# Reordering two places in the engine queues of a fused attention and feed-forward kernel: a weight conversion in the first group, and the last forms of the ninth group

## The chip, the cores and the metric

The kernel runs on one core of a Trainium2 chip. A core has a matrix engine (TensorE, PE in the profile), a vector engine (VectorE, DVE), an activation engine (ScalarE, ACT), a general engine (GpSimd, POOL) and a queue engine (SyncE, SP) that mostly issues transfers. Each engine works off its own list of instructions; semaphores make one engine wait for another. The metric is the device time of one execution in microseconds (us).

## The reference: what is computed

```python
kv  = einsum('bhsd,bhse->bhde', k, v)           # per head, 64 x 64
out = einsum('bhsd,bhde->bhse', q, kv)          # q, k, v: (8, 8, 576, 64)
rms = sqrt(mean(out * out, axis=-1) + 1e-06)
x   = (out / rms * g_norm)  ->  (8*576, 8*64)   # 4608 tokens, 512 wide

h  = x @ w_in                                   # w_in:  512 x 2048
sp = maximum(h, 0) + log1p(exp(-abs(h)))        # softplus
g  = h * erf(sp)
y  = g @ w_out                                  # w_out: 2048 x 512
```

Attention without a softmax, a norm over each head's 64 values, and a feed-forward block with its own activation function. The two weight matrices arrive as 64-bit floats; everything else is 32-bit.

## The kernel before

**Groups.** The 4608 tokens are cut into nine groups of 512. Groups T = 0 to 7 are the first 512 rows of each batch element. What is left of each (64 rows) is gathered in `x_last` and makes the ninth group, T = 8 (`T == B` in the code). For each group the attention is done in four pairs of heads (p = 0 to 3), and the feed-forward block in 16 units of 128 columns of `w_in` (`FC = 16`).

**Attention** (`attention`, from L269) is cut into six pieces: `products` (kv and the transposed q), `apply` (q times kv), `halve` (a split of the squares), `mean` (the mean of squares on PE, then logarithm, exponential and square on ACT, L358 to L360), `norm` (three DVE instructions, L366, L369, L378) and `split`. For T = 8 there are no products; `square` reads `x_last`. The pieces of group T + 1 are placed by hand between the units of group T.

**Forms.** From the second group on, the products are made of cut operands[...]. `thirds` (L424) cuts a tile into an upper form (ACT, L405), a lower form, which is the rest (DVE, L408), and a mix of both (DVE, L411). `product` (L449) then needs 12 matmuls: eight into `n_ps` (upper and lower form for each of four blocks) and four into `m_ps` (the mix). It takes turns over three pairs of PSUM banks, so the result that lay in a pair must be read out before the product three places later writes there.

**First stage, n = 0 to 32** (L644): groups 0 and 1, one unit a step. In group 0 the 64-bit weights are converted. `weights()` (L256) does one step of it: `w_split` of one block (DVE L207 and L216, then ACT L215 and L219), `w_join` of the block before it (DVE L226, L230, L240) and the load of a later block. `due(k)` says whether a conversion is needed soon; `due(1)` asks for one more step in advance than `due(0)`. It is called in two places of a step: with 1 ahead of the attention pieces of that step, which include `norm`, and with 0 after them (L658 and L664). `gates` (L641) multiplies h by erf(softplus(h)). At n = 6 the first pair's `norm` of group 1 comes up.

**Second stage, m = 8 to 36** (L786): groups 2 to 8 in batches of four units. Pass m makes the four hidden products of batch m (`hidden`), then the four result products of batch m - 1 (`result`, L765). Around them it does the following in this order:

- for each of four units i: the hidden product; for the first two, the forms of the gated h of the batch before (`cut_upper` on ACT, `cut_lower` on DVE); then h is copied out of PSUM (ACT L836, and DVE L445 adds the second bank), and softplus (ACT L838);
- the error functions (ACT L842), and, when little is left in `todo`, a load of the softplus table (L843);
- for each of four row blocks j: the result product, which DVE adds to `e` (L440 and L445), and after j = 1 the gates of this batch on DVE (L856, two halves).

The attention pieces wait in the list `todo`; `places` says after which unit or row block each may run (1 to 4 are the units, 5 to 8 the row blocks). m = 31 is the last batch of group 7, in which the last pair of group 8 gets its `mean`, `norm` and `split`. m = 32 is the first batch of group 8, whose first product needs those forms. m = 35 is the last batch and m = 36 only makes results.

[...]

Of the kernel before, what the change touches and what calls it, by code (L numbers as in the profile page):

```python
# [43 lines left out]
AF = mybir.ActivationFunctionType  # L44
# [6 lines left out]
BATCH = 4  # L51
# [5 lines left out]
SHIFT = 4096.0  # L57
# [3 lines left out]
def kernel(  # L61
# [10 lines left out]
    nc = tc.nc  # L72
    P = 128
    B, H, S, D = q.shape
# [30 lines left out]
    def softplus_table():  # L105
        nc.scalar.preload_act_table_set("softplus")  # L106
# [149 lines left out]
    def weights():  # L256

        w_next("split")
        w_next("join")
        w_next("load")  # L260
# [183 lines left out]
    def add(out_, ps):  # L444
        nc.vector.tensor_tensor(out=out_, in0=ps, in1=out_, op=ALU.add)  # L445
# [45 lines left out]
    def w_lower(which, f):  # L491

        t, x, parts = w_new.pop((which, f))
        lower_w(x, *(parts[:, i] for i in range(3)))
        kept = w_kept[which, f] = dram.tile([P, 3, G], FP32, name=f"w_{which}{f}")
        for i in range(3):
            if t is None:
                nc.sync.dma_start(
                    out=kept[:, i].rearrange("p (c f) -> p c f", c=KC), in_=parts[:, i].bitcast(FP32)
                )  # L500
        if t is not None:
            nc.sync.dma_start(out=kept, in_=t.bitcast(FP32))
            if which == "in" and f >= WHOLE:
                w_now[which, f] = [t]

    def hidden(T, f, turns=True):

        w = w_now["in", f].pop(0).rearrange("p i (c f) -> p i c f", c=KC).bitcast(FP32R)
        x = x_forms[T]
        return product(lambda form, c: w[:, form, c], lambda form, c: x[form][:, c], turns)  # L510


    NB = FC // BATCH
# [35 lines left out]
    def unit(name):  # L549
        return gate.tile([P, G], FP32, name=name, tag=name[0])  # L550
# [30 lines left out]
    first_batch, batches = FIRST * NB, NG * NB  # L581
# [5 lines left out]
    def load_parts(which, n):  # L587


        pool = w_out_p if which == "out" and len(w_seq["out"]) > BATCH else w_in_p  # L590
        for _ in range(n):
            if w_seq[which]:
                key = w_seq[which].pop(0)
                t = pool.tile([P, 3, G], FP32, name=f"w_{which}_parts", tag="w")
                nc.sync.dma_start(out=t, in_=w_kept[key])
                w_now.setdefault(key, []).append(t)


    def pieces_of(T):


        steps = [([], [], []) for _ in range(FC)]
        for p in range(NP):
            products, apply, halve, mean, norm, split = attention(T, p)
            f = (BATCH - 1) * (p + 1) if T < FIRST else BATCH * p

            steps[f][2 if T == FIRST or p == 1 else 1].append(products)
            steps[f + 1][1].append(apply)
            steps[f + 2][0].append(halve)
            with_erf = (f + 2) % BATCH == BATCH - 1  # L610

            place = 2 if T < FIRST and p == 0 else 1
            steps[f + 2][place].append(partial(mean, table=not with_erf))
            steps[f + 3][0].append(norm)
            steps[min(f + 4, FC - 1)][0].append(split)
        return steps
# [18 lines left out]
    def due(k):  # L635

        i = w_at["join"] + k
        ahead = 1 if LAG - 2 <= n < LAG + BATCH else 2
        return i < len(w_order) and w_order[i][0] <= n + ahead
# [4 lines left out]
    for n in range(FIRST * FC + 1):  # L644
# [10 lines left out]
        if T < FIRST:  # L655
            if f == 0:
                steps = pieces_of(T + 1)
            if due(1):  # L658
                weights()
            for key in list(w_new)[:2]:  # L660
                w_lower(*key)
            for piece in steps[f][0]:
                piece()
# [13 lines left out]
        if T == FIRST - 1 and f >= WHOLE:  # L677
            n_ps, m_ps = hidden(T, f, turns=False)
# [19 lines left out]
        if T < FIRST:  # L698
            if n == whole:
                old_h = acc.tile([P, BATCH, G], FP32, name="h", tag="e")  # L700
            h = hs[n] = old_h[:, n - whole] if n >= whole else unit("h_sb")
# [51 lines left out]
    def part(h, half):  # L753
        return h[:, :, half * 2 * P : half * 2 * P + 2 * P]

    def cut_upper(h, half):

        t = late_r.tile([P, 3, BATCH, 2 * P], FP32R, name=f"g_forms{half}")
        upper(part(h, half), t[:, 0])
        return t  # L760

    def cut_lower(h, half, t):
        lower(part(h, half), *(t[:, i] for i in range(3)))

    def result(T, b, j, g, w):  # L765

        ps = product(
            lambda form, f: g[j // 2][:, form, f, j % 2 * P : j % 2 * P + P],
            lambda form, f: w[f][:, form],
        )  # L770
        if b == 0:
            if j == 0:
                all_e = wide.tile([P, J, DM], FP32, name="e", tag="a")
                es.update((i, all_e[:, i]) for i in range(J))
            nc.vector.tensor_scalar(
                out=es[j], in0=ps[0], scalar1=SHIFT - 1.0, scalar2=None, op0=ALU.mult
            )
        else:
            add_scaled(es[j], ps[0], SHIFT - 1.0)
        add(es[j], ps[1])  # L780
# [5 lines left out]
    for m in range(first_batch, batches + 1):  # L786
        T, b = divmod(m, NB)
        todo = []
        if T + 1 < NG:
            todo = list(attention(T + 1, b))  # L790
            if b == 0:
                side = late_r if T % 2 == FIRST % 2 else late
                forms = side.tile([P, 3, KC, G], FP32R, name=f"x_forms{(T + 1) % 2}")
                x_forms[T + 1] = [forms[:, i] for i in range(3)]

        def piece():
            if todo:
                todo.pop(0)()


        places = (0, 2, 3, 5, 6, 8)
        if T + 1 == B:
            places = (0, 0, 0, 5, 6, 7)
            if b == NB - 1:

                places, todo[3] = (0, 0, 0, 4, 5, 6), partial(todo[3], table=False)
        elif b == NB - 1:
            places = (0, 2, 3, 5, 6, 7)

        def pieces(place):  # L810
            while todo and places[-len(todo)] <= place:
                todo.pop(0)()

        def fetch(place):
            for which in FETCH[place].split():
                load_parts(which, 1)

        pieces(0)
        g, done = g_next, len(g_next)
        g_next = []  # L820
        if m < batches:

            pool, tag = (acc, "e") if m % 2 else (wide, "b")
            h = pool.tile([P, BATCH, G], FP32, name="h", tag=tag)
            s = gate_r.tile([P, BATCH, G], FP32, name="s", tag="s")
        for i in range(BATCH):
            if m < batches:
                n_ps, m_ps = hidden(T, b * BATCH + i)
            fetch(i)
            if i == 0:  # L830
                for half in range(done, 2):
                    g.append(cut_upper(old_h, half))
            if done <= i < 2:
                cut_lower(old_h, i, g[i])
            if m < batches:
                nc.scalar.activation(h[:, i], n_ps, AF.Copy, scale=SHIFT - 1.0)  # L836
                add(h[:, i], m_ps)
                nc.scalar.activation(s[:, i], h[:, i], AF.Softplus)  # L838
            pieces(i + 1)
        if m < batches:  # L840
            for i in range(2):
                nc.scalar.activation(part(s, i), part(s, i), AF.Erf)  # L842
            if len(todo) < 3:  # L843
                softplus_table()
        T2, b2 = divmod(m - 1, NB)
        w = [w_now["out", b2 * BATCH + f].pop(0).bitcast(FP32R) for f in range(BATCH)]
        for j in range(J):
            result(T2, b2, j, g, w)
            fetch(BATCH + j)
            if b2 == NB - 1:  # L850
                store(T2, j, es.pop(j))
            if j == 1 and m == batches - 1:
                cut_lower(h, 0, g_next[0])

            for half in range(2) if j == 1 and m < batches - 1 else (j,) if j < 2 and m == batches - 1 else ():
                nc.vector.tensor_tensor(  # L856
                    out=part(h, half), in0=part(h, half), in1=part(s, half), op=ALU.mult
                )
            if j == 0 and m == batches - 1:
                g_next.append(cut_upper(h, 0))  # L860
            pieces(BATCH + 1 + j)
        old_h = h
# [33 lines left out]
```

## Time and profile before

| | |
|---|---|
| time, median of 3 runs | 948.07 us (947.21 to 948.4) |
| span of the profiled execution | 945.7 us |
| PE busy | 926.8 us (98%) |
| DVE busy | 740.5 us (78%) |
| ACT busy | 615.7 us (65%) |
| hidden products, n_ps and m_ps from x_forms | 233.2 + 120.0 us on PE |
| result products, n_ps and m_ps from g_forms | 231.2 + 124.2 us on PE |
| table loads on ACT | 44, of 1283 ns |

The rows of a timeline read: start, length, engine, line, operation, output <- inputs, shape, count, and in brackets the idle time of the engine just before, with what ended it. Consecutive instructions of one kind are merged into one row. Starts are measured; the ends of matmuls are modelled and overlap the next, so PE's pace is read from the distance between two starts. "Lnnn" is a line of the code.

### The profile page before, as it was taken

To read this page: it belongs to the slowest core of one execution; us is meant where nothing else is said; L and a number is where in the kernel's file an instruction comes from. 1 tells how busy PE (TensorE), PEld (TensorE's weight loads), DVE (VectorE), ACT (ScalarE), POOL (GpSimd) and SP (SyncE) were. 2 spreads that over 40 slices of the span, in tenths; PEclk is the share of its full clock that TensorE was granted. 3 is DMA by queue.
4 is the path that set the end of the run, shared out by engine and by line. 5 is a ranking of instruction groups with operands and counts; after the bars stand their busy time and mean duration, and the time that the engine had idled before them with its cause. 6 is when DMAs were issued, how large, how long until landed. Compare 5 with 4: busy or idle time off the path is not lost.

```text
span 945.7 us, 11743 instructions
## 1 busy us (share of the span) xinstructions
PE 926.8 (98%) x4272; PEld 683.3 (72%) x4272; DVE 740.5 (78%) x1054; ACT 615.7 (65%) x825; POOL 2.4 (0%) x10
## 2 busy tenths in 40 slices
PE   6999999999999999999999999999999999999998
PEld 4444445665688888888888888888888888878886
DVE  3979958888578788777788888878887877777667
ACT  3889876777666666666666666666666666665552
POOL 1000000000000000000000000000000000000000
PEclk9999999999999999999999999999999999999999
DMA  9856505899699998998899889998896778768872
GB/s 258 282 158 215 169 9 215 310 339 340 219 364 346 317 303 284 315 301 303 275 295 314 303 288 311 312 301 294 293 323 261 265 247 352 284 245 309 335 273 60
DMA packets 111842, 259.78 MB, mean 275 GB/s; under 512 B 43864, under 2 KB 69544, under 8 KB 111784
## 3 DMA queue, kind: packets, MB, share of 16 engines
q1 hardware_dynamic: 110152, 256.73, 78.4%
q10 hardware_dynamic: 1568, 2.29, 0.8%
q8 instruction: 34, 0.56, 0.2%
q14 instruction: 24, 0.20, 0.1%
q0 software_dynamic: 64, 0.00, 0.0%
HBM read 224.40 MB, written 34.60 MB: 274 GB/s over the span
## 4 chain that ended last, share of the span: by engine, by line
PE 88%; ACT 5%; DVE 5%; DMA 1%; issue 1%; DVEq 0%
PE n_ps L462 45%; PE m_ps L462 23%; PE o_ps L520 8%; PE h_ps L691 3%; PE se_ps L325 3%; PE kv_ps L297 2%; PE qt_ps L319 2%; ACT w_e L215 1%; ACT w_m L219 1%; DMA q_sb<-in_q_dram 1%; PE ms_ps L347 1%; PE ms_ps L346 1%; PE ms_ps L351 1%; ACT L103 1%; ACT s_sb L719 1%
## 5 line engine op out<-in xcount | busy, mean ns | idle before, releaser
L462 PE MATMUL n_ps<-x_forms,w_in_parts 128*128 128x512 f32 x896 | 233.2, 402 | 1.6 <-DVE x_forms L408 0.7
L462 PE MATMUL n_ps<-w_out_parts,g_forms 128*128 128x512 f32 x928 | 231.2, 391 | 0.0
L462 PEld LDWEIGHTS n_ps<-w_out_parts,g_forms 128*128 128x128 f32 x928 | 174.2, 188 | 38.4 <-issue 1.7
L462 PEld LDWEIGHTS n_ps<-x_forms,w_in_parts 128*128 128x128 f32 x896 | 166.7, 188 | 45.3 <-issue 9.1
L838 ACT ACTIVATE s<-h 128x512 f32<-128x512 f32 x112 | 71.0, 634 | 180.4 <-DVE h L445 180.4
L445 DVE TENSOR_TENSOR h<-m_ps,h 128x512 f32<-128x512 f32 x116 | 79.8, 688 | 60.9 <-ACT h L836 41.5
L462 PE MATMUL m_ps<-w_out_parts,g_forms 128*128 128x512 f32 x464 | 124.2, 389 | 0.0
L462 PE MATMUL m_ps<-x_forms,w_in_parts 128*128 128x512 f32 x448 | 120.0, 390 | 0.0
L520 PE MATMUL o_ps<-w_out_sb,h_sb 128*128 128x512 f32 x224 | 100.8, 593 | 0.3 <-DVE h_sb L642 0.3
L462 PEld LDWEIGHTS m_ps<-w_out_parts,g_forms 128*128 128x128 f32 x464 | 87.1, 188 | 18.1
L462 PEld LDWEIGHTS m_ps<-x_forms,w_in_parts 128*128 128x128 f32 x448 | 84.1, 188 | 17.7
L445 DVE TENSOR_TENSOR e<-m_ps,e 128x512 f32<-128x512 f32 x116 | 80.3, 692 | 18.3 <-PE m_ps L462 11.2
L440 DVE SCALAR_TENSOR_TENSOR e<-n_ps,e 128x512 f32<-128x512 f32 x88 | 60.3, 686 | 39.6 <-PE n_ps L462 39.6
L520 PEld LDWEIGHTS o_ps<-w_out_sb,h_sb 128*128 128x128 f32 x224 | 42.3, 190 | 48.9 <-issue 46.6
L411 DVE SCALAR_TENSOR_TENSOR g_forms<-g_forms 128x1024 fp32r<-128x1024 f32 x58 | 71.1, 1225 | 2.0
L408 DVE TENSOR_TENSOR g_forms<-h,g_forms 128x1024 fp32r<-128x1024 f32 x58 | 70.6, 1218 | 1.7 <-ACT g_forms L405 1.4
L836 ACT ACTIVATE h<-n_ps 128x512 f32<-128x512 f32 x112 | 65.5, 585 | 3.9 <-PE n_ps L462 3.8
L405 ACT ACTIVATE g_forms<-h 128x1024 fp32r<-128x1024 f32 x58 | 58.8, 1058 | 12.4 <-PE m_ps L462 9.8
L856 DVE TENSOR_TENSOR h<-h,s 128x1024 f32<-128x1024 f32 x56 | 66.0, 1218 | 0.7 <-ACT s L842 0.7
L691 PE MATMUL h_ps<-xT,w_in_sb 128*128 128x512 f32 x144 | 64.9, 594 | 0.8 <-DVE w_in_sb L240 0.6
L106 ACT ACT_TABLE_LOAD x44 | 56.5, 1283 | 0.7
L842 ACT ACTIVATE s<-s 128x1024 f32<-128x1024 f32 x56 | 56.3, 1053 | 0.3
(98 smaller groups left out, 1014.3 us busy)
## 6 DMA issues: line engine op xcount, KB each, us to landing
w_out_parts<-w_out SPq DMA_DIRECT2D x116, 768.0 KB
w_in_parts<-w_in SPq DMA_DIRECT2D x112, 768.0 KB
w_in<-w_new SPq DMA_DIRECT2D x16, 768.0 KB
q_sb<-in_q_dram SPq DMA_DIRECT2D x32, 256.0 KB
w_raw<-in_moe_w_out_dram SPq DMA_DIRECT2D x8, 1024.0 KB
out_dram<-e SPq DMA_DIRECT2D x32, 256.0 KB
k_sb<-in_k_dram SPq DMA_DIRECT2D x28, 287.5 KB
v_sb<-in_v_dram SPq DMA_DIRECT2D x28, 287.5 KB
```

Source lines behind the costliest of these rows:

```text
L106: nc.scalar.preload_act_table_set("softplus")
L405: nc.scalar.activation(high, x, AF.Copy, scale=1.0 + 2.0**-13)
L408: nc.vector.tensor_tensor(out=low, in0=x, in1=high.bitcast(FP32), op=ALU.subtract)
L411: nc.vector.scalar_tensor_tensor(out=both, in0=low.bitcast(FP32), scalar=SHIFT, in1=high.bitcast(FP32), op0=ALU.mult, op1=ALU.add,)
L440: nc.vector.scalar_tensor_tensor(out=out_, in0=ps, scalar=scale, in1=out_, op0=ALU.mult, op1=ALU.add)
L445: nc.vector.tensor_tensor(out=out_, in0=ps, in1=out_, op=ALU.add)
L462: nc.tensor.matmul(ps, lhsT=weights(form, k), rhs=moving(form, k), start=(form == forms[0] and k == 0), stop=(form == forms[-1] and k == 3),)
L520: nc.tensor.matmul(o_ps[j], lhsT=g[:, j * P : j * P + P], rhs=w_out_sb[:, f, :], start=(f == 0), stop=last,)
L691: nc.tensor.matmul(plain[i], lhsT=w_in_sb[:, c, i % FC * P : i % FC * P + P], rhs=xT[T][:, c, :], start=(c == 0), stop=(c == KC - 1),)
L836: nc.scalar.activation(h[:, i], n_ps, AF.Copy, scale=SHIFT - 1.0)
L838: nc.scalar.activation(s[:, i], h[:, i], AF.Softplus)
L856: nc.vector.tensor_tensor(out=part(h, half), in0=part(h, half), in1=part(s, half), op=ALU.mult)
```

## The change

It moves work inside the queues; its aim is that instructions which nothing holds up go ahead of instructions that wait for another engine.

- In step n = 6 of the first stage, `weights()` is called by the rule that before applied only after the attention pieces. So one conversion goes ahead of the first pair's `norm`.
- In pass m = 31, `norm` goes from after the first to after the second row block, and `split` after the third, where it now stands ahead of the load of the softplus table and ahead of the gates. The gates go from after the second to after the third row block.
- In pass m = 32 the first unit's h is copied out before the forms of the batch before are cut.
- The condition for the gates is rewritten. Before, passes with m < batches - 1 gated both halves, m = batches - 1 one half each after the first two row blocks, and m = batches none. Now every pass other than m = batches - 1 takes the last branch.

```diff
-            if due(1):
+
+            if due(0 if n == 2 * (BATCH - 1) else 1):
                 weights()
...
             if b == NB - 1:
 
-                places, todo[3] = (0, 0, 0, 4, 5, 6), partial(todo[3], table=False)
+
+                places, todo[3] = (0, 0, 0, 4, 6, 7), partial(todo[3], table=False)
+                todo[5] = partial(chain, todo[5], softplus_table)
...
+        to_last = m == B * NB - 1
...
+            def evacuate():
+                nc.scalar.activation(h[:, i], n_ps, AF.Copy, scale=SHIFT - 1.0)
+                add(h[:, i], m_ps)
+
+
+            early_copy = i == 0 and m == B * NB
+            if early_copy:
+                evacuate()
...
             if m < batches:
-                nc.scalar.activation(h[:, i], n_ps, AF.Copy, scale=SHIFT - 1.0)
-                add(h[:, i], m_ps)
+                if not early_copy:
+                    evacuate()
                 nc.scalar.activation(s[:, i], h[:, i], AF.Softplus)
...
-            if len(todo) < 3:
+            if len(todo) < 2:
                 softplus_table()
...
-            for half in range(2) if j == 1 and m < batches - 1 else (j,) if j < 2 and m == batches - 1 else ():
+            if m == batches - 1:
+                due_halves = (j,) if j < 2 else ()
+            else:
+                due_halves = range(2) if j == (2 if to_last else 1) else ()
+            if to_last:
+                pieces(BATCH + 1 + j)
+            for half in due_halves:
                 nc.vector.tensor_tensor(
                     out=part(h, half), in0=part(h, half), in1=part(s, half), op=ALU.mult
                 )
```

## The prediction

> **What bounds the kernel now.** I read the page's shares first, then the timeline of TensorE (PE) for the places where it stands still, then the other two engines' timelines at those places.
>
> ```profile
> PE 926.8 (98%) x4272; PEld 683.3 (72%) x4272; DVE 740.5 (78%) x1054; ACT 615.7 (65%) x825; POOL 2.4 (0%) x10
> ```
>
> PE is busy for all but 18.9 us of a 945.7 us span. The table of busy time by stage has it busy for the whole of every stretch from 100 to 250 us and 300 to 750 us, so an edit can pay only where PE stands still. Of the 18.9 us, 8.7 lie in the first 25 us and 4.5 after the last matmul's turn begins to run out (925 us on). The rest is small, and two pieces of it lie beside the change. The first is in group 0:
>
> ```profile
> 64.83 3.60 PE L691 MATMUL h_ps<-xT,w_in_sb 128*128 128x512 f32 x8
> 69.44 0.43 PE L324 MATMUL kv_ps<-qT_last,bd_kv 128*128 128x64 f32 x2 [1.02 <-DVE bd_kv L312]
> ...
> 74.30 3.70 PE L691 MATMUL h_ps<-xT,w_in_sb 128*128 128x512 f32 x8
> ...
> 86.02 0.80 PE L297 MATMUL kv_ps<-v_sb,k_sb 116*64 116x64 f32 x20 [0.29 <-DVE qT L366]
> 86.75 0.33 PE L305 MATMUL kv_ps<-ident,q_last 128*128 128x128 f32 x1
> 87.53 0.66 PE L319 MATMUL qt_ps<-ident,q_sb 128*128 128x128 f32 x4 [0.45 <-DVE xT L378]
> ```
>
> In brackets stands the idle time and what ended it: three times PE waits for VectorE (DVE). What DVE was doing:
>
> ```profile
> 56.03 0.69 DVE L642 TENSOR_TENSOR h_sb<-h_sb,s_sb 128x512 f32<-128x512 f32 x1
> 61.48 0.69 DVE L366 SCALAR_TENSOR_TENSOR qT<-ms_ps,qT 128x512 f32<-128x512 f32 x1 [4.76 <-ACT qT L360]
> ...
> 62.93 0.75 DVE L378 SCALAR_TENSOR_TENSOR xT<-se_ps,gm_col,qT 128x512 f32<-128x512 f32 x1
> 63.60 0.69 DVE L207 TENSOR_SCALAR w_e<-w_raw 128x1024 int32<-128x1024 int32 x1
> ...
> 68.33 0.68 DVE L642 TENSOR_TENSOR h_sb<-h_sb,s_sb 128x512 f32<-128x512 f32 x1
> 68.93 0.45 DVE L312 COPY bd_kv<-kv_ps 64x64 f32<-64x64 f32 x2
> ```
>
> It stood 4.76 us in front of the norm (L366), which needs ScalarE's (ACT's) logarithm, exponential and square. Only then came the weight conversion (L207 to L240, 63.60 to 68.33), and behind it the copy bd_kv that PE waits for. The second place is the first product of group 8:
>
> ```profile
> 840.92 1.54 PE L462 MATMUL n_ps<-x_forms,w_in_parts 128*128 128x512 f32 x6
> 843.18 0.49 PE L462 MATMUL n_ps<-x_forms,w_in_parts 128*128 128x512 f32 x1 [0.72 <-ACT x_forms L405]
> 844.42 0.50 PE L462 MATMUL n_ps<-x_forms,w_in_parts 128*128 128x512 f32 x1 [0.74 <-DVE x_forms L408]
> ```
> ```profile
> 839.17 2.01 ACT L842 ACTIVATE s<-s 128x1024 f32<-128x1024 f32 x2
> 841.20 1.28 ACT L106 ACT_TABLE_LOAD   x1
> 842.50 0.63 ACT L405 ACTIVATE x_forms<-x 128x512 fp32r<-128x512 f32 x1
> ```
>
> The upper form of the last attention piece waits behind a table load on ACT, and its lower form waits on DVE for the gates (two L856, 841.41 to 843.68). The third place is the end:
>
> ```profile
> 937.58 0.69 DVE L445 TENSOR_TENSOR e<-m_ps,e 128x512 f32<-128x512 f32 x1
> 938.19 0.68 DVE L440 SCALAR_TENSOR_TENSOR e<-n_ps,e 128x512 f32<-128x512 f32 x1
> ...
> 941.28 0.69 DVE L445 TENSOR_TENSOR e<-m_ps,e 128x512 f32<-128x512 f32 x1 [0.21 <-PE m_ps L462]
> ```
>
> DVE ends the work at 941.97. It is idle for only 0.71 us between the last two result blocks.
>
> [...] L207 had nothing to wait for at 56.7 and still ran at 63.60, behind the norm. [...] The trace has 1283 ns, and no drain (the load from 841.20 is followed by work at 842.50), so I use 1.28. [...] The row of L856 has 1218.
>
> **The change part by part.**
>
> *Conversion ahead of the norm (n = 6).* Compared with before, only DVE's order changes: L207, L216, L226, L230, L240 go in front of L366, L369, L378. The five start 0.60, 0.60, 1.14, 1.25 and about 1.14 us apart, 4.73 in all, and fit the hole: from 56.7 to 61.4, while the norm can start at 61.48. Does something else hold them? The two joins need ACT's L215 and L219 of the split before (54.91 to 57.0, done by the time L226 comes up at 57.9). The raw block was loaded three conversions earlier (issue at 42.70). Nothing holds them, and the norm isn't later. Behind the norm, the gates and bd_kv no longer have 4.73 us in front of them: bd_kv then waits for PE's own kv_ps (ends 64.4) and is done at about 65.1, where PE needs it at 68.4. ACT gains as well: L215 of the new split waited 1.57 us for L207 and now follows its table load at 62.75. Following both queues on to n = 9, ACT's square ends at about 81.7 instead of 85.25, and the norm of the second pair ends at about 83.9 instead of 87.47. PE would reach kv_ps at about 84.5 and qt_ps at 85.3. All three waits fall away. What they cost I take from PE's pace against the same pair of rows without a wait: L691 to L324 4.61 against 3.43 (1.18); the rows after it 0.10 and, up to the L691 of 74.30, 0.24; slower first matmuls after that 0.11; L691 to L297 3.89 against 3.52 (0.37); L305 to L319 0.78 against 0.16 (0.62). Sum 2.6. The bounds are 1.0 (the first wait alone) and 2.7; I take 2.5. PE shows no idle time from there to 250 us, and DVE and ACT, fed by PE, move with it.
>
> *Last forms of group 8 (m = 31 and 32).* No instruction is added there. On DVE the second result block (e, L440 and L445) goes ahead of the norm, into its 2.63 us wait for ACT; the norm still runs from 837.89 to 840.1. Then come the third block (to 841.4), the forms, the gates, the fourth block. On ACT the upper form follows the error functions directly: 841.20 to 841.83, and the table load comes after it. DVE's lower form then runs from 841.86 to 842.54, the third form to 843.27. PE wants the upper at 842.28, the lower at 842.51 and the third form at about 843.5: a loss of 0.1 instead of now 0.90 and 1.01 by pace, with 0.3 more for the slower matmuls after it (the next product's halves come 1.94 apart, not 1.81). So 2.2 less 0.1: 2.1 gained. What is pushed back: the gates end at about 845.5 (before: 843.7) and the fourth block's first half at 846.15. Its PSUM bank is the one that the third product of m = 32 writes from 846.4 on, 0.25 us of slack. The early copy of h serves that: the copy sits on ACT at 843.1, before the conversions of the gates, and its addition on DVE ends at 847.6. After that the additions and copies that free banks come 0.5 to 1 us ahead of PE (third copy 854.1, wanted at 854.6). Bounds for the gain: 1.0, if these slacks are eaten, and 2.2.
>
> *Gates in the last pass (m = 36).* The rewritten condition leaves out the old bound m < batches - 1, so the last pass multiplies the old h by s once more. Two L856-like instructions stand on DVE after the second result block, at 938.19. A pair takes 2.27 (841.41 to 843.68). Queued behind them are the third and fourth blocks and their stores. Third block 940.46, fourth 941.85 to 943.33, where the end was 941.97: 1.36 later, 2.27 less the 0.91 us of idle time that it absorbs. Nothing hides it, and the last store follows directly. Bounds 1.1 and 1.6 (the last two stores come closer together).
>
> Sum: 2.5 + 2.1 - 1.4 = 3.2 us. 948.07 - 3.2 = 944.9.
>
> **The rivals.**
> - *The group-8 gain is eaten by bank waits.* PE meets late evacuations in m = 32, and only 0.6 remain: 948.07 - 2.5 - 0.6 + 1.4 = 946.4. For it: slacks of 0.25 and 0.5 us in an order that I worked out by hand. Against: each is positive, and DVE idles 1.18 us twice before additions there.
> - *The group-0 gain is given back in group 1*, where the transfers of the cut weights fill the DMA engines (mean share 0.95 from 200 to 250 us) and PE waits 0.31 for DVE at 250.77: 948.07 - 2.1 + 1.4 = 947.4. Against: the DMA engines idle from 135 to 145 us and run at 0.40 from 250 to 260, so that stream is started by PE and would start earlier too.
> - *Both gains go and the added gates stay:* 948.07 + 1.4 = 949.5. It needs both rivals at once, in full; the removed waits are on PE itself, which speaks against it.
>
> **How the numbers follow.** Forecast 0.78, first rival 0.09, second 0.09, slower 0.04. The forecast's bounds are 948.07 - 2.7 - 2.2 + 1.1 = 944.3 and, with a gain of 1.0 in one of the two places and 1.6 at the end, about 946.4. Half a microsecond for the spread of the three times (947.21 to 948.4) makes 943.8 to 946.9, which holds the first rival too and leaves out 0.13. Faster by over 0.2% means below 946.2: nearly all of the forecast and some of the first rival, 0.80. Within: 0.16. Slower: 0.04.
>
> **What would show it.** Right: no PE wait for bd_kv near 68 us nor for L366 and L378 near 84; DVE's wait before L366 in group 0 near zero; the first L462 row of group 8 in one piece of eight; two gates on DVE some 5 us before the end, with the last addition starting about 5.1 us after the start of the second block's last addition (now 3.7). Wrong: a new PE wait on L440, L445 or the copy of h in m = 32; PE idle near 250 us grown by 2 us; or gates at the end that fall into idle time.

## The result and the profile after

| | before | after |
|---|---|---|
| time, median | 947.81 us (947.21 to 948.4, 4 runs) | 944.32 us (943.95 to 944.94, 4 runs) |
| span of the profiled execution | 945.7 us | 942.4 us |
| PE busy | 926.8 us | 924.8 us |
| DVE busy | 740.5 us | 742.6 us |

The changed kernel is 3.5 us faster; the ratio of the times is 0.9964, with a 95% interval of 0.9947 to 0.9981. The number of matmuls is the same in the two executions (4272), and DVE has 2.1 us more work. In the table of the kernel before, the 44 table loads are those of one line, L106 (softplus); with those ahead of the logarithm (L103, 33 times) and of the error function (L842 28 and L726 8 times in the kernel before) there are 113, of 1283 ns each, in both kernels. PE's busy time isn't a measure of the gain: it falls by 2.0 us with the same matmuls, since their ends are modelled and PE is 0.66 us less busy in the first 25 us, ahead of any difference between the kernels.

Three places account for it. In each I measure the distance between two rows of the same execution, because the start of the kernel is not equally long each time (last section). The first is group 0, PE's timeline after:

```profile
55.93 1.02 PE L351 MATMUL ms_ps<-qT,mean_w 128*128 128x512 f32 x2
...
64.98 3.60 PE L692 MATMUL h_ps<-xT,w_in_sb 128*128 128x512 f32 x8
68.41 0.33 PE L324 MATMUL kv_ps<-qT_last,bd_kv 128*128 128x64 f32 x2
...
72.93 3.60 PE L692 MATMUL h_ps<-xT,w_in_sb 128*128 128x512 f32 x8
...
84.18 0.80 PE L297 MATMUL kv_ps<-v_sb,k_sb 116*64 116x64 f32 x20
...
85.08 0.60 PE L319 MATMUL qt_ps<-ident,q_sb 128*128 128x128 f32 x4
85.51 3.60 PE L520 MATMUL o_ps<-w_out_sb,h_sb 128*128 128x512 f32 x8
```

All brackets are gone. Before, the stretch that I measure lies between these two rows:

```profile
55.78 1.02 PE L351 MATMUL ms_ps<-qT,mean_w 128*128 128x512 f32 x2
...
88.02 3.60 PE L520 MATMUL o_ps<-w_out_sb,h_sb 128*128 128x512 f32 x8
```

L692 (L691 before) to L324 is 3.43 us where it was 4.61. From the mean's matmuls in front (L351) to the L520 that follows qt_ps it takes 32.24 us before and 29.58 after: 2.66 gained. The three brackets of before add up to 1.76 only. A bracket counts from the modelled end of the matmul before it, and without a wait that end lies 0.07 to 0.17 us behind the next start (64.98 + 3.60 against 68.41), so each bracket misses that much. Some matmuls just after a wait are slower: the L691 at 74.30 takes 3.54 us to the next row (77.84), and 3.43 after. And there is a fourth wait, which stands on the weight load (PEld) of the L691 at 74.30, before:

```profile
74.30 0.30 PEld L691 LDWEIGHTS h_ps<-xT,w_in_sb 128*128 128x128 f32 x2 [0.91 <-DVE w_in_sb L240]
```

PE waits there for the weight itself, the end of the next conversion (L240, 73.02 to 74.24 on DVE). From the L520 ahead of it to this L691 it is 3.67 us before (70.63 to 74.30), and 3.43 after (69.50 to 72.93). DVE's timeline after shows why the waits are gone:

```profile
55.96 0.68 DVE L642 TENSOR_TENSOR h_sb<-h_sb,s_sb 128x512 f32<-128x512 f32 x1
56.56 0.68 DVE L207 TENSOR_SCALAR w_e<-w_raw 128x1024 int32<-128x1024 int32 x1
...
60.15 1.23 DVE L240 TENSOR_TENSOR w_out_sb<-w_e,w_m 128x1024 f32<-128x1024 f32 x1
61.42 0.69 DVE L366 SCALAR_TENSOR_TENSOR qT<-ms_ps,qT 128x512 f32<-128x512 f32 x1
...
63.55 0.68 DVE L642 TENSOR_TENSOR h_sb<-h_sb,s_sb 128x512 f32<-128x512 f32 x1
64.60 0.46 DVE L312 COPY bd_kv<-kv_ps 64x64 f32<-64x64 f32 x2 [0.37 <-PE kv_ps L297]
```

The conversion fills the 4.76 us in which DVE stood, the norm still runs at 61.4, and the copy bd_kv now waits for PE and no longer PE for it. The next conversion moves up as well: its L207 is at 65.09 where it was at 69.42.

The second place is the first product of group 8. PE, then ACT, then DVE, after:

```profile
838.42 1.98 PE L462 MATMUL n_ps<-x_forms,w_in_parts 128*128 128x512 f32 x8
840.25 1.09 PE L462 MATMUL m_ps<-x_forms,w_in_parts 128*128 128x512 f32 x4
841.17 2.00 PE L462 MATMUL n_ps<-x_forms,w_in_parts 128*128 128x512 f32 x8
...
843.91 1.98 PE L462 MATMUL n_ps<-x_forms,w_in_parts 128*128 128x512 f32 x8
```
```profile
836.60 2.01 ACT L856 ACTIVATE s<-s 128x1024 f32<-128x1024 f32 x2
838.51 0.61 ACT L405 ACTIVATE x_forms<-x 128x512 fp32r<-128x512 f32 x1
839.15 1.28 ACT L106 ACT_TABLE_LOAD   x1
```
```profile
839.16 0.69 DVE L408 TENSOR_TENSOR x_forms<-x,x_forms 128x512 fp32r<-128x512 f32 x1 [0.24 <-ACT x_forms L405]
839.89 0.69 DVE L411 SCALAR_TENSOR_TENSOR x_forms<-x_forms 128x512 fp32r<-128x512 f32 x1
840.50 2.35 DVE L876 TENSOR_TENSOR h<-h,s 128x1024 f32<-128x1024 f32 x2
```

Eight matmuls in one row, where before six, one and one stood with 0.72 and 0.74 us between them. The upper form now precedes the table load, the other forms precede the gates. From this product to the third one it takes 7.68 us before (840.92 to 848.60) and 5.49 after (838.42 to 843.91): 2.19 gained. The row of the third one before:

```profile
848.60 1.98 PE L462 MATMUL n_ps<-x_forms,w_in_parts 128*128 128x512 f32 x8
```

The third is the end. PE's last row before and after, then DVE after:

```profile
940.17 1.07 PE L462 MATMUL m_ps<-w_out_parts,g_forms 128*128 128x512 f32 x4
```
```profile
935.49 1.07 PE L462 MATMUL m_ps<-w_out_parts,g_forms 128*128 128x512 f32 x4
```
```profile
932.88 0.69 DVE L445 TENSOR_TENSOR e<-m_ps,e 128x512 f32<-128x512 f32 x1
933.49 2.35 DVE L876 TENSOR_TENSOR h<-h,s 128x1024 f32<-128x1024 f32 x2
...
937.94 0.69 DVE L445 TENSOR_TENSOR e<-m_ps,e 128x512 f32<-128x512 f32 x1
```

The two gates of the last pass stand in front of the last two result blocks, and the waits for PE there (0.71 and 0.21 us) are gone. From PE's last m_ps to the last addition it takes 1.11 us before (940.17 to 941.28) and 2.45 after (935.49 to 937.94): 1.34 lost.

The sum is 2.66 + 2.19 - 1.34 = 3.51, and the medians differ by 3.49. That the two agree so closely is luck. The three profiled kernels without the conversion's move take 32.02 to 32.24 us for the stretch of group 0, and those with all of it 29.57 or 29.58, so the gain there is 2.4 to 2.7. In group 8 it is 7.62 to 7.70 without the new order and 5.49 to 5.57 with it: 2.05 to 2.21 gained. The traces thus give 3.1 to 3.5 us, and the spans of the two executions differ by 3.3.

### The profile page after: what moved, and what is told of

Same layout as the page of the kernel before. It is cut to its first block, busy times and chain, and to the rows that moved or that the text cites. A ratio compares the mean times of both kernels' runs of the same rounds, so it can differ in the third digit from the quotient of the medians.

```text
span 942.4 us, 11743 instructions
## 1 busy us (share of the span) xinstructions
PE 924.8 (98%) x4272; PEld 683.4 (73%) x4272; DVE 742.6 (79%) x1056; ACT 615.6 (65%) x825; POOL 2.4 (0%) x10
## 4 chain that ended last, share of the span: by engine, by line
PE 92%; DVE 4%; DMA 2%; ACT 1%; issue 0%; SPq 0%; DVEq 0%
PE n_ps L462 45%; PE m_ps L462 22%; PE o_ps L520 10%; PE h_ps L692 6%; PE se_ps L325 3%; PE kv_ps L297 2%; PE qt_ps L319 2%; DMA w_raw<-in_moe_w_in_dram 1%; PE ms_ps L351 1%; DMA v_sb<-in_v_dram 1%; DVE h L876 1%; DVE e L445 1%; PE ms_ps L346 1%; PE ms_ps L347 1%; PE kv_ps L324 1%; DVE e L440 0%
## 5 line engine op out<-in xcount | busy, mean ns | idle before, releaser
L520 PE MATMUL o_ps<-w_out_sb,h_sb 128*128 128x512 f32 x224 | 100.8, 593 | 0.3 <-DVE h_sb L642 0.3
L520 PEld LDWEIGHTS o_ps<-w_out_sb,h_sb 128*128 128x128 f32 x224 | 42.3, 190 | 48.9 <-issue 46.6
L876 DVE TENSOR_TENSOR h<-h,s 128x1024 f32<-128x1024 f32 x58 | 68.3, 1218 | 0.7 <-ACT s L856 0.7
L692 PE MATMUL h_ps<-xT,w_in_sb 128*128 128x512 f32 x144 | 64.9, 594 | 0.7 <-DVE w_in_sb L240 0.6
L106 ACT ACT_TABLE_LOAD x44 | 56.5, 1283 | 0.8
```

The costliest lines, as they stand in the source:

```text
L520: nc.tensor.matmul(o_ps[j], lhsT=g[:, j * P : j * P + P], rhs=w_out_sb[:, f, :], start=(f == 0), stop=last,)
L692: nc.tensor.matmul(plain[i], lhsT=w_in_sb[:, c, i % FC * P : i % FC * P + P], rhs=xT[T][:, c, :], start=(c == 0), stop=(c == KC - 1),)
L876: nc.vector.tensor_tensor(out=part(h, half), in0=part(h, half), in1=part(s, half), op=ALU.mult)
```

## The experiments

The theory: three places, each priced by PE's pace there (at the end by DVE's list), which add up. The rivals: the gains are given back later, or new waits take their place. In the first four kernels the median of before is 947.69 us (24 runs), in the next four 947.80 (45 runs), in the last two 947.78 (9 runs). The changed kernel was timed only beside the 947.81 of the result, so differences to it go across series; where I give one, the distance in the trace is the better measure.

**The conversion alone** (the kernel before with this line):

```diff
-            if due(1):
+            if due(0 if n == 2 * (BATCH - 1) else 1):
```

> The kernel before with the conversion ahead of the norm at n = 6 and nothing else. Theory (the parts add up, each read from PE's idle time at its own place): 2.5 us faster than before, PE's waits near 69, 86 and 87.5 us gone, everything after 90 us moved by 2.5 us, the two waits in the first product of group 8 still 0.7 us each. Rival (the lead is given back in group 1, where the transfers are dense): under 1 us faster, with PE idle time grown near 250 us.

Measured: 945.31 us, 2.4 faster; ratio 0.9974 (0.9965 to 0.9984). PE goes from L351 at 56.27 to the L520 at 85.85 in 29.58 us, as in the changed kernel. Near 250 us PE waits 0.30, as before. The waits in group 8 are untouched:

```profile
840.99 0.50 PE L462 MATMUL n_ps<-x_forms,w_in_parts 128*128 128x512 f32 x1 [0.72 <-ACT x_forms L405]
842.24 0.50 PE L462 MATMUL n_ps<-x_forms,w_in_parts 128*128 128x512 f32 x1 [0.74 <-DVE x_forms L408]
```

So the lead that PE wins before 90 us reaches the end, and the rival falls. All the traces agree on this: from the L520 behind qt_ps to the first product of group 8 it takes 752.86 to 753.16 us in all twelve profiled kernels, with the move and without it.

**The forms alone** (the changed kernel with `due(1)` and without the last gates):

```diff
-            if due(0 if n == 2 * (BATCH - 1) else 1):
+            if due(1):
...
-                due_halves = range(2) if j == (2 if to_last else 1) else ()
+                due_halves = range(2) if m < batches and j == (2 if to_last else 1) else ()
```

> The kernel before with the new order of norm, forms, table, gates and early copy in m = 31 and 32, without the conversion's move and without gates in the last pass. Theory: 2.2 us faster than before, PE's three waits in group 0 as before. Rival (late evacuations take the place of the removed waits): 0.6 us or less.

Measured: 945.77 us, 1.9 faster; ratio 0.9982 (0.9974 to 0.9991). The first three products of group 8 take 5.55 us from start to start (841.35 to 846.90), against 7.68 before. No PE wait stands there. The three in group 0 are still there: 0.80, 0.29 and 0.45, against 1.02, 0.29 and 0.45 before. From the third product to PE's last m_ps it takes 91.57 or 91.58 us in all twelve profiled kernels, so no late evacuation costs PE anything behind it.

**The last gates alone** (the kernel before with):

```diff
-            for half in range(2) if j == 1 and m < batches - 1 else (j,) if j < 2 and m == batches - 1 else ():
+            for half in range(2) if j == 1 and m != batches - 1 else (j,) if j < 2 and m == batches - 1 else ():
```

> The kernel before with only the two gates added in the last pass (they multiply an old h that nothing reads). Theory: 1.35 us slower than before, the last two result blocks behind the gates on DVE. Rival (the gates fall into idle time of DVE or behind the latency of the last stores): within 0.3 us of before.

Measured: 949.08 us, 1.4 slower; ratio 1.0019 (1.0010 to 1.0029). The last m_ps starts at 940.95, and DVE's rows are

```profile
938.95 2.35 DVE L856 TENSOR_TENSOR h<-h,s 128x1024 f32<-128x1024 f32 x2
...
943.40 0.69 DVE L445 TENSOR_TENSOR e<-m_ps,e 128x512 f32<-128x512 f32 x1
```

so 2.45 us from the last m_ps to the last addition, as in the changed kernel.

**The changed kernel without the last gates** (second hunk of the forms' diff alone):

> The changed kernel without the gates in the last pass. Theory: 1.35 us faster than the changed kernel (about 943.0 us), 4.7 us faster than before. Rival (the gates cost nothing at the end): the same as the changed kernel.

Measured: 943.52 us, 4.2 faster than before; ratio 0.9960 (0.9947 to 0.9972). From the last m_ps (936.14) to the last addition it is 1.11 us again, with DVE waiting for PE:

```profile
936.34 0.69 DVE L440 SCALAR_TENSOR_TENSOR e<-n_ps,e 128x512 f32<-128x512 f32 x1 [0.71 <-PE n_ps L462]
937.25 0.69 DVE L445 TENSOR_TENSOR e<-m_ps,e 128x512 f32<-128x512 f32 x1 [0.21 <-PE m_ps L462]
```

Its time is 0.8 below the changed kernel's, where 1.35 was expected. The trace shows 1.34; the five runs lie between 942.7 and 945.49, so the times can't tell 0.8 from 1.34, and by themselves can't tell this kernel from the changed one. By its trace it is the better version of the two. The parts measured alone, 2.4 + 1.9 = 4.3, agree with the 4.2 of both together.

**Without the early copy** (the changed kernel with `early_copy = False`):

> The changed kernel with the first unit of m = 32 copied out in the old place, behind the conversions of the gates. Prediction's reading (the early copy keeps the banks clear): a PE wait for an addition or a copy in m = 32, up to 1 us slower than the changed kernel. Rival (the banks are wanted late enough anyway, since the fourth hidden product asks for the bank only at 8.2 us after the first): no PE wait, the same time within 0.3 us.

Measured: 944.69 us, 3.1 faster than before; ratio 0.9969 (0.9960 to 0.9979). The changed kernel has 0.9964, so no difference can be told. PE doesn't wait in m = 32. DVE and PE:

```profile
849.07 0.68 DVE L445 TENSOR_TENSOR h<-m_ps,h 128x512 f32<-128x512 f32 x1
```
```profile
849.13 1.98 PE L462 MATMUL n_ps<-x_forms,w_in_parts 128*128 128x512 f32 x8
850.94 1.07 PE L462 MATMUL m_ps<-x_forms,w_in_parts 128*128 128x512 f32 x4
```

The first unit's second bank is read out by 849.75, and the fourth product, the next to use it, writes there from 850.94. Even behind the conversions of the gates (g_forms) there is 1.2 us left. The first three products take 5.55 us, within the range of the kernels that have the early copy. The rival was right; the early copy brings nothing that these runs can see.

**Only DVE's order in group 8, or only ACT's.** First, the table load again ahead of the upper form:

```diff
-                todo[5] = partial(chain, todo[5], softplus_table)
...
-            if len(todo) < 2:
+            if len(todo) < 3:
                 softplus_table()
```

> The changed kernel with the softplus table again ahead of the last upper form on ACT; DVE's order as changed. Theory (both queues have to be cleared, and what is left of the delay is what each queue still adds): upper form 1.28 us later, PE waits about 0.6 us for it and about 0.5 us for the lower form, some 1.2 us slower than the changed kernel. Rival (only DVE's order counts): the same time.

Measured: 946.12 us, 1.7 faster than before; ratio 0.9982 (0.9975 to 0.9989), so some 1.8 us slower than the changed kernel. PE's rows:

```profile
841.39 0.50 PE L462 MATMUL n_ps<-x_forms,w_in_parts 128*128 128x512 f32 x1 [0.72 <-ACT x_forms L405]
842.12 0.50 PE L462 MATMUL n_ps<-x_forms,w_in_parts 128*128 128x512 f32 x1 [0.22 <-DVE x_forms L408]
```

The step from this product to the next is 4.23 us (839.15 to 843.38), where the changed kernel has 2.75: 1.48 lost, where some 1.2 was expected. Second, the gates again ahead of the lower form, on DVE:

```diff
-            if to_last:
-                pieces(BATCH + 1 + j)
             for half in due_halves:
```

> The changed kernel with the gates of m = 31 again ahead of the last lower form on DVE; ACT's order as changed. Theory: no PE wait for the upper form, about 1.8 us of PE wait for the lower one, some 2 us slower than the changed kernel: nearly the whole gain of this place. Rival (only the table on ACT counts): the same time.

Measured: 946.49 us, 1.3 faster than before; ratio 0.9991 (0.9982 to 0.9999), some 2.2 us slower than the changed kernel.

```profile
842.61 0.50 PE L462 MATMUL n_ps<-x_forms,w_in_parts 128*128 128x512 f32 x1 [1.72 <-DVE x_forms L408]
```

The same step is 4.73 us (839.15 to 843.88), 1.98 lost. In this kernel the wait for ACT is gone, and the wait for DVE has grown from 0.74 to 1.72: the two stood one behind the other, and taking away the first alone only shows more of the second. The two orders bring 0.2 (ACT's alone) and 0.7 us (DVE's alone) of the 2.19; the rest needs both. The norm's later place, behind the second row block, stands in both kernels; what it brings by itself is not shown.

**Four gates in the last pass:**

```diff
-            for half in due_halves:
+            for half in list(due_halves) * (2 if m == batches else 1):
```

> The changed kernel with four gate instructions in the last pass in place of two (the additional ones multiply an old h that nothing reads). Theory (the first pair costs 2.27 less 0.91 us of idle time, a second one finds no idle time left): 2.27 us slower than the changed kernel, about 946.6 us. Rival (each pair costs the same 1.36): 1.36 us slower.

Measured: 947.15 us; ratio to before 0.9993 (0.9984 to 1.0001), 2.8 us slower than the changed kernel by the medians. The last m_ps starts at 936.73, and DVE shows

```profile
934.73 4.62 DVE L876 TENSOR_TENSOR h<-h,s 128x1024 f32<-128x1024 f32 x4
...
941.45 0.69 DVE L445 TENSOR_TENSOR e<-m_ps,e 128x512 f32<-128x512 f32 x1
```

4.72 us from the last m_ps to the last addition, 2.27 more than with two gates. The first pair costs 1.34, since it takes up the idle time; the second costs its whole length. This is what the theory said, though the medians lie 0.6 above it.

**Half of the conversion ahead.** Both kernels are without the last gates, so they compare with 943.52. At n = 6, only the split, or only the join, goes ahead of the norm:

```diff
-            if due(0 if n == 2 * (BATCH - 1) else 1):
+            if due(1):
                 weights()
+            if n == 2 * (BATCH - 1):
+                w_next("split")                        # or: w_next("join"), w_next("load")
             for key in list(w_new)[:2]:
                 w_lower(*key)
             for piece in steps[f][0]:
                 piece()
+            if n == 2 * (BATCH - 1):
+                w_next("join"), w_next("load")         # or: w_next("split")
```

> The changed kernel without the last gates, and with only the split of the conversion (L207, L216) ahead of the norm at n = 6; the join (L226 to L240) goes behind it. DVE's copy bd_kv is then 3.5 us later than in the full move, at about 68.2 us, just before PE wants it; ACT's L215 doesn't wait. Theory (bd_kv in time is what counts first, ACT's lead second): no PE wait or under 0.3 us, about the time of the kernel without the last gates (943.5 us). Rival (PE needs DVE free by the whole 4.7 us): some 1 us slower than that.

Measured: 944.57 us; ratio to before 0.9966 (0.9953 to 0.9979). From L351 (56.45) to the L520 (87.26) it is 30.81 us, 1.23 more than in the full move. The expectation was wrong, and its rival was right on the size. PE, ACT and DVE in this kernel:

```profile
85.25 0.80 PE L297 MATMUL kv_ps<-v_sb,k_sb 116*64 116x64 f32 x20 [0.27 <-DVE qT L366]
...
86.77 0.66 PE L319 MATMUL qt_ps<-ident,q_sb 128*128 128x128 f32 x4 [0.45 <-DVE xT L378]
```
```profile
69.39 1.15 ACT L215 ACTIVATE w_e<-w_e,exp_col 128x1024 int32<-128x1024 int32 x1 [2.47 <-DVE w_e L207]
```
```profile
68.18 0.45 DVE L312 COPY bd_kv<-kv_ps 64x64 f32<-64x64 f32 x2
68.66 0.69 DVE L207 TENSOR_SCALAR w_e<-w_raw 128x1024 int32<-128x1024 int32 x1
```

bd_kv is in time, as expected, and PE's first wait is gone. But the next conversion's split (L207) starts at 68.66, and ACT waits 2.47 us for it. ACT's list after it runs without a pause up to the second pair's square, which ends 28.03 us after L351 (25.78 in the changed kernel), and with it come both waits of the second pair. They cost 1.01 of the 1.23. The other 0.22 is lost at 73.56, where PE waits for the weight (w_in_sb, L240), as before.

> The changed kernel without the last gates, and with only the join (L226 to L240) ahead of the norm at n = 6; the split (L207, L216) goes behind it, so ACT's L215 waits for it again as before (1.57 us). bd_kv is ready at about 66 us. Theory: no PE wait for bd_kv; ACT's chain to the norm of the second pair ends about 1.4 us later than in the full move, so PE may wait some 0.3 us at qt_ps near 85 us; 0 to 0.4 us slower than the kernel without the last gates. Rival (ACT's order carries the gain): 1 us or more slower.

Measured: 943.58 us; ratio to before 0.9958 (0.9943 to 0.9973), the same as the full move within what can be told. L351 (55.47) to the L520 (85.42) is 29.95 us, 0.37 more than in the full move, within the 0 to 0.4 expected:

```profile
84.93 0.66 PE L319 MATMUL qt_ps<-ident,q_sb 128*128 128x128 f32 x4 [0.16 <-DVE xT L378]
```

Here the next split starts on DVE 10.05 us after L351. In the changed kernel it is 9.16, and with only the split ahead 12.21. So the rival named for the split alone had the size but not the reason: here 3.5 of the 4.7 us go ahead, and PE loses 0.37. The two kernels together show what the 2.66 us are made of: bd_kv in time for the first wait, and for the rest an early *next* conversion. Its split lets ACT get ahead, for the second pair's waits, and its join gives PE the weight in time.

## Why the prediction was right

- *What bounds the kernel.* It rested on PE being the limit everywhere but at short stops (busy for 926.8 of 945.7 us). The conversion alone and the forms alone confirm it: what was won at 70 to 90 us is still there at the end, 850 us later. The rival of group 1 had the right observation (dense transfers: the DMA engines' mean share from 200 to 250 us is 0.95 before and 0.93 after), but they moved along with PE: their first issue (L502) is at 148.07 before and at 145.57 after, 60.05 and 60.06 us behind the L520 that follows qt_ps, and PE's wait near 250 us is 0.31 and 0.30.
- *Conversion ahead of the norm.* Predicted 2.5 (sum of the pace 2.6), measured 2.66 between the two traces, 2.4 to 2.7 over all of them, and 2.4 by the time of that part alone. The second pair's norm was to end at about 83.9; it ends at 83.95 (83.20 + 0.75). Both halves of the step, DVE's and ACT's lead, were in the prediction. Two things it didn't name. The 0.24 that it counts up to the L691 of 74.30 is a wait of its own, for the converted weight, so four waits fell away and not three. And ACT's lead depends on the following conversion: the prediction followed the queues and got the right end, but the expectation for the split alone left this out and missed by about 1 us.
- *Last forms.* Predicted 2.1, measured 2.19 in the trace, 1.9 by the time of the part alone. The loss of 0.1 at the lower form was too much: the step is 2.75 us where the steady one is 2.72. The bank of the fourth result block was to be read out 0.25 us before the third product writes there; it is 0.46 (843.45 and 843.91). The table load was counted as 1.28 us with nothing behind it, and that held: the load at 839.15 is followed by work at 840.44.
- *The early copy.* The prediction counted it as what keeps the banks clear. That was wrong, without effect on the sum: the kernel without it has no wait. The bank that was tight, that of the fourth result block, isn't freed by this copy, and the one that is freed is wanted 8.2 us after the first product.
- *Gates in the last pass.* Predicted 1.36 as 2.27 less 0.91 of idle time (the waits of 0.71 and 0.21 before the last two additions); measured 1.34, and the doubled gates show the 2.27 for a pair that finds no idle time.
- *The sum.* Predicted 3.2 us and 944.9, measured 3.5 and 944.32. Between the two traces the terms differ from the predicted ones by 0.16, 0.09 and 0.06, all in the same direction, which is the 0.3. That is no more than one execution differs from the next: over all traces the sum is 3.1 to 3.5. Of the 0.6 us by which the absolute time came out lower, 0.26 is the median of before, which moved from 948.07 to 947.81 with a fourth run.

## What to carry to other kernels

Where an engine takes its list in order, as DVE did here before (L207, with nothing to wait for, ran at 63.60, behind the norm that had waited until 61.48), look for an instruction that waits with others behind it that wait for nothing; moving those ahead cost nothing here, where they fitted the hole (4.73 us of work in 4.76; no longer move was run). Then follow both queues further: part of the gain came one conversion later (1.23 of the 2.66 us were lost when only the split went ahead). When a late operand crosses two engines, clear both lists: here one alone brought 0.2 or 0.7 of 2.2 us. And check a rewritten condition at both ends of its loop: 1.3 us of the gain went to two instructions in the last pass whose result nobody reads. Last, the brackets of PE's rows understate a wait here: those removed add up to 3.22 us, and by pace 4.85 were gained.

## What was not expected of the hardware

The start of the kernel varies more than several of the effects here. All these kernels have the same program up to the first long run of matmuls (h_ps), and in the profiled executions it began between 27.61 and 30.62 us (28.00 before, 27.96 after), with PE waiting 7.2 to 9.2 us in all for the first v_sb transfers. So one profile's span can't settle a difference of 1 us.

Distances within one trace are better, but not all to the same degree. Where PE runs without a wait they repeat closely: the stretch of group 0 took 29.57 or 29.58 us in the seven kernels with the whole move, whose starts differ by up to 2.7 us. Where something waits, they don't: the same stretch took 32.02, 32.07 and 32.24 us in the three kernels without the move, whose first wait is 0.80, 0.85 and 1.02 us. And from the first h_ps to the L351 of group 0, where the program is the same in all twelve, it took 27.78 to 28.43 us.
